# Attention feeding a feed-forward block: the first two chunks interleaved, the weights decoded in that order, GpSimd's early work given to TensorE and VectorE

## The chip, the core and the metric

The kernel runs on one core of one Trainium2 chip. The metric is the device time of one execution in microseconds (us). A core has five engines with an instruction stream each: TensorE (PE in the profile, its weight loads PEld), VectorE (DVE), ScalarE (ACT), GpSimd (POOL) and SyncE (SP), which here issues the transfers from and to memory (DMA). They wait for one another through semaphores. SBUF is the on-chip memory; PSUM is the memory that matmuls write, eight banks of 128 partitions by 2 KB.

## The reference

```python
# q, k, v: [8 batches, 8 heads, 576 positions, 64], float32
q_d, k_d, v_d = (a.reshape(B, H, 144, 4, D).mean(axis=3) for a in (q, k, v))
out_up = np.repeat(sm_attn(q_d, k_d, v_d), 4, axis=2)          # "down": pooled attention
mask = np.abs(pos[:, None] - pos[None, :]) < 4                 # "local": 7 neighbours
attn = softmax(np.where(mask, scale * q @ k.T, -1e9))
x = (out_up + attn @ v).transpose(0, 2, 1, 3).reshape(4608, 512)
h = x @ w_in                                                   # 512 x 2048
g = np.maximum(h, 0.0) + alpha * np.minimum(h, 0.0)
out = g @ w_out                                                # 2048 x 512
```

The weights `w_in`, `w_out` and `alpha` are float64 in memory.

## The kernel before

**Feed-forward part.** The 4608 tokens are cut into 18 chunks of 256. Each chunk has 8 steps, of 256 of the 2048 hidden columns each, so that there are 144 steps; step 8c+i is part i of chunk c. `h_step` computes h in a `ps_h` bank with 24 matmuls of 128x256 (each operand is split in a high and a low part: xh·wih, xh·wil, xl·wih). ScalarE (`t`, L651) and VectorE (`t`, L654) apply the two slopes, ScalarE copies the high part `gh` (L656), GpSimd subtracts to get the low part `gl` (L97). `out_step` adds 12 matmuls of 128x512 into two output banks (L690) that stay with the chunk for its 8 steps, and are then copied by ScalarE to `sg` and stored. h steps run two ahead of out steps (`AH = 2`); `t`, `gh` and `gl` have two buffers each. In this text "t8" is the VectorE part of step 8, and so on.

**Weights.** A float64 arrives as two int32 words. `decode` turns a 128x512 piece into a float32 (`temp`): Abs on ScalarE, then on VectorE a clamp (L153), a shift (L154) and two combining operations (L155, L156). ScalarE then writes the high part (`wih`, `woh`), and the low part is a subtraction (`wil`: VectorE L210, or GpSimd L97 for 5 of 16 pieces by `POOL_LO`; `woh` and `wol` with a sign, VectorE L204). `load_weights` walks four groups n of 512 hidden columns, w_in before w_out in each: 32 pieces. Group 3 is late: its buffers come free when the attention of batch 0 is done.

**Attention.** Batch 0 is done up front by `pair(hp)` for four pairs of heads, with the scores on TensorE. Batches 1 to 7 run in the shadow of the feed-forward steps, as units u = 3 to 23 of 192 tokens. `local(u)` multiplies shifted k by q and reduces, on VectorE (L551, L553), from a copy `qp` of q in PSUM bank q (copied by ScalarE, L548); it keeps the probabilities and the running sum `lb` in PSUM bank l, and multiplies by v and adds (L596, L598), which gives `x`; then come transposes on TensorE, an addition of the pooled part (`xf`) and the split in high and low parts. `down(b, hp)` is the pooled attention of a pair of heads: loads `ld` (three buffers), additions on GpSimd (L100), small matmuls and softmax.

**PSUM.** `ps_o` 2 banks (output sums), `ps_h` 2, q 1, l 1, d 2.

**Order.** The program is written chunk by chunk, with as many attention steps issued between two feed-forward steps as the tokens need that are wanted next; a list scheduler then sets the order on each engine by readiness in its own timeline, with priorities (`high_priority`: the work behind h by `HP`, `pair` by `PP`, decode by `DP`). On an engine instructions run strictly in that order. Transfers are issued by SP in its own order, each waiting for its buffer.

## Time and profile before

| | us |
|---|---|
| runs | 1144.88, 1130.85, 1134.6 |
| median | 1134.6 |
| profiled execution, its own time | 1138.52 |
| its span in the profile | 1136.7 |

| engine | busy us | share of the span |
|---|---|---|
| PE | 1005.7 | 88% |
| DVE | 861.4 | 76% |
| POOL | 526.4 | 46% |
| ACT | 454.7 | 40% |

The mean granted TensorE clock of the profiled execution is 0.926. From 359 us on TensorE is busy 734.65 of 777.7 us. The first t runs at 111.9 us; by 359 us the weights are decoded and the first 27 steps or so have begun. In the timeline t8 begins at 178.7, t16 at 251.0 and t24 at 320.4 us; unit 3's products begin at 160.7 us, unit 4's at 224.7 us. A row of the windows view gives, for a stretch, each engine's busy us with the number of instructions, the granted clock, the DMA share and GB/s. In a timeline row stand start, duration, engine, line, operation, output<-inputs, size, and in brackets how long the engine had been idle and for whom.

### The profile page before, as it was taken

To read this page: it belongs to the slowest core of one execution; us is meant where nothing else is said; L and a number is where in the kernel's file an instruction comes from. 1 tells how busy PE (TensorE), PEld (TensorE's weight loads), DVE (VectorE), ACT (ScalarE), POOL (GpSimd) and SP (SyncE) were. 2 spreads that over 40 slices of the span, in tenths; PEclk is the share of its full clock that TensorE was granted. 3 is DMA by queue.
4 is the path that set the end of the run, shared out by engine and by line. 5 is a ranking of instruction groups with operands and counts; after the bars stand their busy time and mean duration, and the time that the engine had idled before them with its cause. 6 is when DMAs were issued, how large, how long until landed. Compare 5 with 4: busy or idle time off the path is not lost.

```text
span 1136.7 us, 17891 instructions
## 1 busy us (share of the span) xinstructions
PE 1005.7 (88%) x6402; PEld 879.8 (77%) x6402; DVE 861.4 (76%) x1467; ACT 454.7 (40%) x1223; POOL 526.4 (46%) x633
## 2 busy tenths in 40 slices
PE   5857797898768999889999999989999989999995
PEld 5646675696657898777888888878888878899994
DVE  7999496597847889678878988779887778895110
ACT  5767344242323443333444334344343425333221
POOL 4787474333434644544555543555537244333221
PEclk9756889798968999899999999999999989999998
DMA  8944612222222222221223222323222212100000
GB/s 181 240 150 145 189 43 86 65 83 76 66 92 77 87 100 87 92 87 65 80 95 109 85 80 89 105 76 101 88 92 82 96 58 78 54 19 19 1 20 19
DMA packets 57503, 98.26 MB, mean 86 GB/s; under 512 B 19910, under 2 KB 25286, under 8 KB 57414
## 3 DMA queue, kind: packets, MB, share of 16 engines
q1 hardware_dynamic: 57414, 97.12, 27.1%
q8 instruction: 50, 0.82, 0.3%
q14 instruction: 39, 0.32, 0.1%
HBM read 87.67 MB, written 9.44 MB: 85 GB/s over the span
## 4 chain that ended last, share of the span: by engine, by line
PE 53%; DMA 20%; DVE 11%; POOL 6%; SPq 4%; issue 3%; ACT 2%; ACTq 0%; POOLq 0%; DVEq 0%
PE o L690 26%; PE h L642 22%; DMA ldk<-in_k 10%; DMA q<-in_q 4%; DMA ldq<-in_q 3%; POOL gl L97 2%; SPq L348 2%; DVE temp L155 1%; SPq L499 1%; POOL ldv L100 1%; DVE temp L153 1%; PE pv L266 1%; DVE temp L156 1%; PE xp L607 1%; DMA raw<-in_moe_w_out 1%
## 5 line engine op out<-in xcount | busy, mean ns | idle before, releaser
L97 POOL TENSOR_TENSOR gl<-t,gh 128x512 fp32r<-128x512 f32 x144 | 187.0, 1301 | 238.5 <-ACT gh L656 221.3
L654 DVE SCALAR_TENSOR_TENSOR t<-h,sign,t 128x256 f32<-128x256 f32 x288 | 125.6, 478 | 165.1 <-ACT t L651 159.3
L690 PE MATMUL o<-woh,gl 128*128 128x512 f32 x576 | 193.7, 414 | 45.1 <-POOL gl L97 45.0
L651 ACT ACTIVATE t<-h,slope 128x256 f32<-128x256 f32 x288 | 120.3, 469 | 244.4 <-PE h L642 159.4
L642 PE MATMUL h<-xh,wih 128*128 128x256 f32 x1152 | 201.1, 291 | 1.0 <-DVE t L654 0.7
L690 PE MATMUL o<-woh,gh 128*128 128x512 f32 x576 | 190.2, 407 | 10.3 <-ACT gh L656 10.3
L642 PE MATMUL h<-xh,wil 128*128 128x256 f32 x1152 | 194.3, 288 | 1.0 <-DVE wil L210 1.0
L690 PE MATMUL o<-wol,gh 128*128 128x512 f32 x576 | 191.2, 409 | 0.0
L642 PE MATMUL h<-xl,wih 128*128 128x256 f32 x1152 | 188.0, 285 | 0.0
L642 PEld LDWEIGHTS h<-xh,wih 128*128 128x128 f32 x1152 | 174.0, 196 | 14.4 <-DVE t L654 2.4
L690 PEld LDWEIGHTS o<-woh,gl 128*128 128x128 f32 x576 | 110.4, 195 | 75.8 <-POOL gl L97 51.7
L642 PEld LDWEIGHTS h<-xh,wil 128*128 128x128 f32 x1152 | 163.1, 194 | 1.9 <-DVE wil L210 1.2
L642 PEld LDWEIGHTS h<-xl,wih 128*128 128x128 f32 x1152 | 159.9, 192 | 0.3
L656 ACT CAST gh<-t 128x512 fp32r<-128x512 f32 x144 | 89.4, 621 | 148.5 <-PE o L690 78.6
L551 DVE TENSOR_TENSOR qk<-k,qp 128x768 f32<-128x768 f32 (+1 forms) x126 | 135.0, 1081 | 0.0
L553 DVE TENSOR_REDUCE ls<-qk 128x12 f32<-128x768 f32 (+1 forms) x126 | 133.5, 1080 | 0.2
L690 PEld LDWEIGHTS o<-wol,gh 128*128 128x128 f32 x576 | 111.1, 195 | 24.9 <-issue 0.2
L690 PEld LDWEIGHTS o<-woh,gh 128*128 128x128 f32 x576 | 102.3, 194 | 25.2 <-ACT gh L656 10.5
L598 DVE TENSOR_TENSOR lb<-lb,pv 128x384 f32<-128x384 f32 x210 | 117.9, 562 | 4.0
L100 POOL TENSOR_TENSOR ldk<-ldk 72x256 f32<-72x256 f32 x56 | 45.2, 808 | 153.7 <-DMA ldk<-in_k 143.3
L596 DVE TENSOR_TENSOR pv<-v,lb 128x1152 f32<-128x1152 f32 x84 | 96.8, 1152 | 2.5
L100 POOL TENSOR_TENSOR ldq<-ldq 72x256 f32<-72x256 f32 x56 | 42.8, 774 | 80.6 <-DMA ldq<-in_q 80.4
(146 smaller groups left out, 1194.3 us busy)
## 6 DMA issues: line engine op xcount, KB each, us to landing
k<-in_k SPq DMA_DIRECT2D x41, 384.0 KB
v<-in_v SPq DMA_DIRECT2D x41, 384.0 KB
raw<-in_moe_w_in SPq DMA_DIRECT2D x16, 512.0 KB
raw<-in_moe_w_out SPq DMA_DIRECT2D x16, 512.0 KB
ldq<-in_q SPq DMA_DIRECT2D x56, 144.0 KB
ldk<-in_k SPq DMA_DIRECT2D x56, 144.0 KB
ldv<-in_v SPq DMA_DIRECT2D x56, 144.0 KB
q<-in_q SPq DMA_DIRECT2D x42, 192.0 KB
```

The source lines that it names most:

```text
L97: nc.gpsimd.tensor_tensor(o, a, b, op=ALU.subtract)
L100: nc.gpsimd.tensor_tensor(o, a, b, op=ALU.add)
L348: nc.sync.dma_start(qk[hp][:, i, :, e, :], bass.AP(src.tensor, (2 * hp + e) * HEAD, [[512, 72], [64, 8], [1, 64]]))
L551: nc.vector.tensor_tensor(pr[:, :nd], window(kt, half, d0, nd), qp.unsqueeze(1).to_broadcast([128, nd, 2, 192]), op=ALU.mult)
L553: nc.vector.tensor_reduce(out=s[:, half, d0:d0 + nd, :].rearrange("p a b -> p (a b)"), in_=pr[:, :nd].rearrange("p a h (t d) -> p (a h t) ...
L596: nc.vector.tensor_tensor(pr[:, :nd], window4(vt, half, d0, nd), prob(half, d0, nd), op=ALU.mult)
L598: nc.vector.tensor_tensor(acc, acc, pr[:, i], op=ALU.add)
L642: nc.tensor.matmul(ph[:, j], w[:, m, 128 * o:128 * o + 128], x[:, m, :], start=(i == 0), stop=(i == 11))
L651: nc.scalar.activation(t[:, j], ph[:, j], AF.Copy, scale=slope[:, f:f + 1])
L654: nc.vector.scalar_tensor_tensor(t[:, j], ph[:, j], sign[:, f:f + 1], t[:, j], op0=ALU.mult, op1=ALU.max)
L656: nc.scalar.copy(gh, t)
L690: nc.tensor.matmul(po, g[:, j, 128 * m:128 * m + 128], wo[w][n][:, o, :], start=(f == 0 and i == 0), stop=(f == NF - 1 and i == 2))
```

## The change

**Order of steps.** `PAIRED = 2`: the steps run 0, 8, 1, 9, 2, 10, ..., 7, 15, and from 16 on as before. Both chunks use each piece of weight when it is there. Chunk 1's two output sums need banks of their own meanwhile: they are put in banks q and l, which units' `local` uses too. Unit 3 (`UB = {3: 'sx'}`) reads q straight from SBUF in its products, without a copy in bank q; its `lb` stays in bank l.

**Weights.** Loaded and decoded by step, 256 hidden columns at a time, in the order in which the steps ask for them: w_in piece 0 (`i0`), w_out piece 0 (`o0`), `i1`, `o1`, ... Pieces 0 to 5 are made with batch 0's attention, 6 and 7 late. Three raw buffers are used in turn. A w_in transfer now has runs of 2 KB (256 float64), before 4 KB. All `wil` subtractions are VectorE's. `HOLD = 5`: the first three `ld` transfers of the downs come behind a tiny VectorE copy that reads `wol` of piece 5.

**Batch 0's attention.** The sums over 4 neighbours of q and k (VectorE for two pairs, GpSimd for two) and of v (GpSimd) become accumulating matmuls: 16 instead of 4 transposes for q and k, 16 instead of 4 for the pooled product with v, per pair; the v tiles get four buffers. The multiplication of the probabilities with 1/sum (128x630) and the low part of x (8 pieces of 128x256 or so) move from GpSimd to VectorE. The fourth pair's exp is done like the other three's (subtract on VectorE, one exp on ScalarE, reduce on VectorE). `GATE`, small VectorE copies that delayed raw loads, is gone. All pairs have priority 1, and the decode none.

The diff, cut to its core (removed code that the functions above show is left out):

```diff
@@ -46,31 +46,21 @@
...
-FQ = 'vvpp'
-FV = 'pppp'
-FSUB = 'vvvv'
-FMUL = 'pppp'
-FLO = 'pppp'
-FEXP = 'vvva'
-SEQ = '00001111'
-UB = {}
-GATE = (-1, -1, 2, 3)
+UB = {3: 'sx'}
...
-DP = (1, 100, 1, 1)
-PP = (1, 1, 250, 250)
-POOL_LO = (1, 5, 1, 1)
-ORDER = 'a0 w w a1 w w a2 b0 w w a3 b1 w w b2 b3'
-WIDE = ()
+PP = (1, 1, 1, 1)
+ORDER = 'a0 i0 a1 o0 a2 i1 b0 a3 b1 o1 i2 b2 b3'
+PAIRED = 2
+HOLD = 5
...
+    raws, turns = {}, [0, 0]
+    weights_temp = []
+
+    def load_raw(which, fp):
+        n = fp // 2
+        if which == 1 and n == 3:
+            pool, tag, bufs = pools[0], ("prod", "vt")[fp % 2], 2
+            raw = [pool.tile([128, 1, 512, 2], I32, tag=tag, name=f"raw1_{fp}{c}", bufs=bufs) for c in range(2)]
+        elif which == 1:
+            t = one.tile([128, 2, 512, 2], I32, tag=f"slot{turns[0] % 3}", name=f"raw1_{fp}")
+            raw = [t[:, c:c + 1] for c in range(2)]
+        else:
+            slot = turns[0] % 3 if n < 3 else 2 + fp % 2
+            t = one.tile([128, 2, 2, 256, 2], I32, tag=f"slot{slot}", name=f"raw0_{fp}")
+            raw = [t[:, c] for c in range(2)]
+        turns[0] += 1
+        src = (w_in, w_out)[which].bitcast(I32)
+        for c in range(2):
+            if which == 0:
+                nc.sync.dma_start(raw[c].rearrange("p k a b -> p k (a b)"),
+                                  bass.AP(src.tensor, 256 * c * 2 * DF + 512 * fp, [[2 * DF, 128], [256 * DF, 2], [1, 512]]))
+            else:
+                row = 256 * fp + 128 * c
+                nc.sync.dma_start(raw[c].rearrange("p k a b -> p (k a b)"), src[row:row + 128, :])
+        raws[which, fp] = raw
+
+    def weight_tiles(which, n):
+        if n == 0 or (wi, wo)[which][0][n] is not None:
+            return
+        w = (wi, wo)[which]
+        for i, x in enumerate("hl"):
+            tag = f"slot{2 * which + i}" if n == 3 else f"spare{8 - 4 * n + 2 * which + i}"
+            w[i][n] = one.tile([128, 4, 512], F32R, tag=tag, name=f"w{'io'[which]}{x}{n}")
+
+    def make(which, fp):
+        n, half = divmod(fp, 2)
+        if not weights_temp:
+            weights_temp.append(one.tile([128, 4, 512], I32, tag="slot3", name="temp"))
+        weight_tiles(which, n)
+        w = (wi, wo)[which]
+        for c, raw in enumerate(raws.pop((which, fp))):
+            if n < 3:
+                t = weights_temp[0][:, turns[1] % 4]
+            else:
+                t = pools[0].tile([128, 512], I32, tag=("x", "xf")[turns[1] % 2], name=f"temp{which}{fp}{c}")
+            turns[1] += 1
+            hi, lo = raw[:, :, :, 1], raw[:, :, :, 0]
+            if which == 0:
+                t = t.rearrange("p (k a) -> p k a", k=2)
+                wh, wl = (w[i][n][:, 2 * c:2 * c + 2, 256 * half:256 * half + 256] for i in range(2))
+                decode(t, hi, lo)
+                nc.scalar.copy(wh, f32(t))
+                nc.vector.tensor_tensor(wl, f32(t), f32(wh), op=ALU.subtract)
+            else:
+                t = t.rearrange("p (k a) -> p k a", k=1)
+                f = 2 * fp + c
+                wh, wl = (w[i][n][:, f % 4:f % 4 + 1] for i in range(2))
+                decode(t, hi, lo)
+                sg = sign[:, f:f + 1]
+                nc.scalar.activation(wh, f32(t), AF.Copy, scale=sg)
+                nc.vector.scalar_tensor_tensor(wl, f32(t), sg, f32(wh), op0=ALU.mult, op1=ALU.subtract)
 
...
+                if held:
+                    nc.vector.tensor_copy(ld[:, 0, 0, 0:1], held.pop())
                 nc.sync.dma_start(ld.rearrange("p g f d -> p (g f d)"),
...
-            vt[hp] = st.tile([72, 2, 8, 64], F32, tag="vt", name=f"fv{hp}", bufs=2)
+            vt[hp] = st.tile([72, 2, 8, 64], F32, tag="vt", name=f"fv{hp}", bufs=4)
...
-                            nc.tensor.transpose(ps[:, (2 * x + g) * 72:(2 * x + g) * 72 + 72], sums[x][:, g],
-                                                ident[:72, :72])
+                            o = ps[:, (2 * x + g) * 72:(2 * x + g) * 72 + 72]
+                            for t in range(4):
+                                nc.tensor.matmul(o, qk[hp][:, x, 4 * g + t].rearrange("p h d -> p (h d)"), ident[:72, :72],
+                                                 start=(t == 0), stop=(t == 3))
...
             if EM[hp] == "b":
                 th = yield from down_probs(0, hp, sd)
             mx = one.tile([128, NWIN], F32, tag="lmx", name=f"fmx{hp}")
             sm = one.tile([128, NWIN], F32, tag="lsm", name=f"fsm{hp}")
...
-            ENG[FMUL[hp]].tensor_tensor(p, p, rs.unsqueeze(2).to_broadcast([128, NWIN, KEYS]), op=ALU.mult)
+            nc.vector.tensor_tensor(p, p, rs.unsqueeze(2).to_broadcast([128, NWIN, KEYS]), op=ALU.mult)
...
-                    nc.tensor.matmul(po[r, 0:144].rearrange("p (b a) -> p b a", b=3), vd[:, g, 64 * e:64 * e + 64],
-                                     pr, start=(g == 0), stop=(g == 1))
+                    for t in range(4):
+                        nc.tensor.matmul(po[r, 0:144].rearrange("p (b a) -> p b a", b=3), vt[hp][:, e, 4 * g + t, :],
+                                         pr, start=(g == 0 and t == 0), stop=(g == 1 and t == 3))
...
-                    ENG[FLO[hp]].tensor_tensor(lo, xs, f32(hi), op=ALU.subtract)
+                    nc.vector.tensor_tensor(lo, xs, f32(hi), op=ALU.subtract)
...
     def new_outs(c):
-        if c == 1 and SEQ != "00001111":
+        if 0 < c < PAIRED:
             outs[c] = outs.get(c) or [bank(kind, f"o1_{kind}") for kind in "ql"]
...
+        todo = [(w, fp) for fp in range(NP) for w in range(2)]
         for step in ORDER.split():
-            if step == "w":
...
-        while next(wl) != "late":
-            pass
+        for fp in range(NP - 2):
+            for which in range(2):
+                if (which, fp) not in raws:
+                    load_raw(which, fp)
+                make(which, fp)
...
+    for which in range(2):
+        for fp in (NP - 2, NP - 1):
+            load_raw(which, fp)
+    for which in range(2):
+        for fp in (NP - 2, NP - 1):
+            make(which, fp)
+    held.extend(f32(wo[1][HOLD // 2][0:72, 2 * (HOLD % 2) + 1, c:c + 1]) for c in range(LDB))
...
+    order = [NP * c + fp for fp in range(NP) for c in range(PAIRED)] + list(range(PAIRED * NP, NS))
+    for c in range(PAIRED):
+        new_outs(c)
```

Three places of the instruction order. The numbers behind names count tiles; `h8_1936` is h of step 8, `qk3_05` unit 3's product of half 0.

First, VectorE in the middle of unit 3. Before:

```order
L551 TENSOR_TENSOR qk3_05_1257<-k3_1199,qp3_0_1209 128x768
L156 SCALAR_TENSOR_TENSOR temp321_1099<-raw321_1096,temp321_1099 128x512
L654 SCALAR_TENSOR_TENSOR t7_1882<-h7_1857,sign_78,t7_1882 128x256 x2
L553 TENSOR_REDUCE ls3_1208<-qk3_05_1257 128x12
L204 SCALAR_TENSOR_TENSOR wol3_1075<-temp311_1088,sign_78,woh3_1074 128x512
L204 SCALAR_TENSOR_TENSOR wol3_1075<-temp321_1099,sign_78,woh3_1074 128x512
L551 TENSOR_TENSOR qk3_10_1278<-k3_1199,qp3_1_1276 128x1152
L153 TENSOR_SCALAR temp331_1108<-temp331_1108 128x512
L654 SCALAR_TENSOR_TENSOR t8_1961<-h8_1936,sign_78,t8_1961 128x256 x2
```

After, the end of unit 3 and the t's behind it:

```order
L578 TENSOR_TENSOR pv3_11_1541<-v3_1253,lb3_1397 128x1152
L580 TENSOR_TENSOR lb3_1397<-lb3_1397,pv3_11_1541 128x384 x3
L578 TENSOR_TENSOR pv3_14_1562<-v3_1253,lb3_1397 128x768
L281 TENSOR_REDUCE dnb1_3_1659<-s1_3_1655 96x3
L580 TENSOR_TENSOR lb3_1397<-lb3_1397,pv3_14_1562 128x384 x2
L582 TENSOR_TENSOR x3_1442<-lb3_1397,pv6_3_1_1425 128x2x3x64
L287 RECIPROCAL drs1_3_1661<-dsm1_3_1660 96x3
L634 SCALAR_TENSOR_TENSOR t3_1859<-h3_1834,sign_78,t3_1859 128x256 x2
L634 SCALAR_TENSOR_TENSOR t11_1930<-h11_1905,sign_78,t11_1930 128x256 x2
L597 TENSOR_TENSOR xf3_0_1741<-xp3_0_1736,od1_1235 128x4x4x16
L597 TENSOR_TENSOR xf3_0_1741<-xp3_0_1736,od1_1235 128x2x4x16 x2
L634 SCALAR_TENSOR_TENSOR t4_2007<-h4_1982,sign_78,t4_2007 128x256 x2
```

Unit 3's first products (`qk3_05`, `qk3_10`) had t7 and t8 and decode operations among them. Now all of unit 3, up to `x3` of both halves, stands ahead of t3, t11 and t4, and the decode is over before it.

Second, TensorE at the first out step of chunk 1 that uses bank l. Before, the sums of step 8 (`o1_0`, `o1_1`):

```order
L642 MATMUL h12_2233<-xh1_382,wih2_930 128x256 x4
L642 MATMUL h12_2233<-xh1_382,wil2_932 128x256
L690 MATMUL o1_0_2122<-woh0_82,gh8_1962 128x512
L690 MATMUL o1_0_2122<-wol0_83,gh8_1962 128x512
L690 MATMUL o1_0_2122<-woh0_82,gl8_1963 128x512
L690 MATMUL o1_0_2122<-woh0_82,gh8_1962 128x512
L690 MATMUL o1_0_2122<-wol0_83,gh8_1962 128x512
L690 MATMUL o1_1_2123<-woh0_82,gh8_1962 128x512
```

After:

```order
L251 MATMUL qkT1_3_1600<-ident_73,s2k1_3_1582 128x72 x2
L262 MATMUL s1_3_1655<-kd1_3_1653,qd32_84 96x144 x3
L670 MATMUL o1_l_1166<-woh0_82,gh8_1227 128x512
L670 MATMUL o1_l_1166<-wol0_83,gh8_1227 128x512
L670 MATMUL o1_l_1166<-woh0_82,gl8_1228 128x512
L670 MATMUL o1_l_1166<-woh0_82,gh8_1227 128x512
L670 MATMUL o1_l_1166<-wol0_83,gh8_1227 128x512
```

Step 8's out matmuls stood behind h11 and part of h12. Now the second half of them (`o1_l`) stands behind the small matmuls of the fourth `down`, and the h steps behind it in the same stream; `o1_l` takes the bank that `lb3` had.

Third, ScalarE where unit 4's q is copied (`qp4_0`, to bank q). Before:

```order
L656 CAST gh8_1962<-t8_1961 128x512
L203 ACTIVATE woh3_1074<-temp331_1108,sign_78 128x512
L651 ACTIVATE t9_2038<-h9_2013,slope_79 128x256 x2
L548 COPY qp4_0_1769<-q4_1342 128x384
L281 ACTIVATE dp1_3_1614,dsm1_3_1612<-s1_3_1607,dnb1_3_1611 96x144 x3
L283 ACTIVATE dsm1_3_1612<-dsm1_3_1612 96x3
L287 ACTIVATE dp1_3_1614<-dp1_3_1614,drs1_3_1613 96x144 x3
```

After:

```order
L675 COPY sg0_0_2614<-o0_0_1163 128x512
L675 COPY sg0_1_2617<-o0_1_1164 128x512
L631 ACTIVATE t17_2668<-h17_2643,slope_79 128x256 x2
L636 CAST gh17_2669<-t17_2668 128x512
L675 COPY sg1_0_2689<-o1_q_1165 128x512
L675 COPY sg1_1_2692<-o1_l_1166 128x512
L530 COPY qp4_0_1817<-q4_1390 128x384
L631 ACTIVATE t18_2767<-h18_2742,slope_79 128x256 x2
L636 CAST gh18_2768<-t18_2767 128x512
```

`qp4_0` stood behind t9. Now it stands behind t17 and behind the copies `sg1_0` and `sg1_1` of chunk 1's finished sums, of which the first is the last reader of bank q.

More of the change, by code (lines that the diff above doesn't have):

```diff
@@ L100, in add @@
         nc.gpsimd.tensor_tensor(o, a, b, op=ALU.add)
+    NS = NCHUNK * NF // 2
+    NP = NF // 2
     ident = const.tile([128, 128], F32, name="ident")
@@ L145, in tile_attention_moe, with decode @@
             w[i][0] = const.tile([128, 4, 512], F32R, name=f"{name}{x}0")
-    def decode(dst, raw):
-        hi, lo = raw[:, :, :, 1], raw[:, :, :, 0]
+    def decode(dst, hi, lo):
         nc.scalar.activation(f32(dst), f32(hi), AF.Abs)
@@ L216, in tile_attention_moe @@
     od = {}
+    held = []
     qd32 = const.tile([128, 3, 96], F32, name="qd32")
```

113 lines of the change are left out of this document (11 added, 102 removed).

## Prediction

> **What bounds the kernel now.** I read the page's row of transfers first (GB/s in 40 slices of 28.4 us), then a windows view cut at t0, unit 3, unit 4, t24 and 359 us.
>
> ```profile
> GB/s 181 240 150 145 189 43 86 65 83 76 66 92 77 87 100 87 92 87 65 80 95 109 85 80 89 105 76 101 88 92 82 96 58 78 54 19 19 1 20 19
> ```
>
> ```profile
> 13.40:111.90 98.50, 68.89 (x450) 57.16 (x449) 96.82 (x164) 66.32 (x186) 68.64 (x52) 0.69 0.68 177
> 111.90:160.70 48.80, 38.09 (x210) 32.10 (x211) 32.26 (x46) 20.07 (x50) 30.43 (x35) 0.79 0.45 143
> 160.70:224.70 64.00, 50.08 (x292) 42.04 (x292) 42.83 (x71) 22.95 (x63) 25.33 (x27) 0.87 0.21 71
> 224.70:320.40 95.70, 83.82 (x518) 73.53 (x517) 80.55 (x133) 32.93 (x88) 37.37 (x49) 0.93 0.22 75
> 320.40:359.00 38.60, 23.85 (x135) 20.80 (x134) 17.15 (x35) 11.13 (x36) 16.20 (x23) 0.73 0.23 78
> 359.00:1136.70 777.70, 734.65 (x4772) 648.11 (x4770) 586.62 (x1008) 295.99 (x794) 340.64 (x421) 0.98 0.22 73
> ```
>
> (Columns: stretch and length, then PE, PEld, DVE, ACT, POOL busy, clock, DMA share, GB/s.) From 359 us TensorE is busy 734.65 of 777.7 us (94%): what comes sooner or later to t24 goes on to the end nearly whole. Up to t0 VectorE is full (96.82 of 98.5), so the start is VectorE's. Between, neither is full, and waits decide. From some steps behind t24 on the order on the engines is the same in both kernels. So I predict when t24 (320.4 us) comes, in five stages.
>
> **A: up to t0.** VectorE's decode operations side by side, as a timeline and as groups:
>
> ```profile
> 13.40 0.43 DVE L153 TENSOR_SCALAR temp<-temp 128x512 f32<-128x512 f32 x1 [2.94 <-ACT temp L152]
> 13.87 0.43 DVE L154 TENSOR_SCALAR temp<-temp 128x512 int32<-128x512 int32 x1
> 14.33 0.69 DVE L155 SCALAR_TENSOR_TENSOR temp<-raw,temp 128x512 int32<-128x512 int32 x1
> 15.42 0.68 DVE L156 SCALAR_TENSOR_TENSOR temp<-raw,temp 128x512 int32<-128x512 int32 x1
> 16.83 1.28 POOL L97 TENSOR_TENSOR wil<-temp,wih 128x512 fp32r<-128x512 f32 x1 [4.31 <-ACT wih L206]
> 16.93 1.73 DVE L155 SCALAR_TENSOR_TENSOR temp<-raw,temp 128x512 int32<-128x512 int32 x1
> 18.80 0.65 DVE L442 TENSOR_TENSOR fp<-fs,fmx 128x490 f32<-128x490 f32 x1
> 22.36 0.68 DVE L210 TENSOR_TENSOR wil<-temp,wih 128x512 fp32r<-128x512 f32 x1
> 22.96 0.41 DVE L410 TENSOR_TENSOR fs2q<-fqk 72x256 f32<-72x256 f32 x1
> 23.29 0.80 DVE L451 TENSOR_REDUCE fsm<-fp 128x9 f32<-128x630 f32 x1
> 114.41 0.74 DVE L204 SCALAR_TENSOR_TENSOR wol<-temp,sign,woh 128x512 fp32r<-128x512 f32 x1
> ```
>
> ```profile
> L153 DVE TENSOR_SCALAR temp<-temp 128x512 f32<-128x512 f32 x32 | 22.6, 709 | 11.3 <-ACT temp L152 11.3
> L154 DVE TENSOR_SCALAR temp<-temp 128x512 int32<-128x512 int32 x32 | 22.8, 713 | 0.3
> L155 DVE SCALAR_TENSOR_TENSOR temp<-raw,temp 128x512 int32<-128x512 int32 x32 | 27.4, 857 | 0.2
> L156 DVE SCALAR_TENSOR_TENSOR temp<-raw,temp 128x512 int32<-128x512 int32 x32 | 27.5, 864 | 0.1
> L204 DVE SCALAR_TENSOR_TENSOR wol<-temp,sign,woh 128x512 fp32r<-128x512 f32 x16 | 15.0, 950 | 8.2 <-ACT woh L203 8.2
> L210 DVE TENSOR_TENSOR wil<-temp,wih 128x512 fp32r<-128x512 f32 x11 | 10.9, 995 | 0.0
> ```
>
> L155 took 0.69 alone and 1.73 when it began 0.10 us behind a GpSimd operation of 1.28. The groups sum to 126.2 us. At the single durations they would be 32 x (0.43+0.43+0.69+0.68) + 16 x 0.74 + 11 x 0.68 = 90.7. The excess of 35.5 us is what GpSimd at its side costs. In the new order GpSimd has nothing between its first masks and gl0, so this excess goes for the 24 of 32 pieces that are made before t0: 35.5 x 24/32 = 27; I take 24, since some of the excess comes behind t0.
>
> Added to VectorE: four 128x630 multiplications (0.65 x 630/490 = 0.84 each, 3.4), eight low parts (0.48 each by t's group below, 3.8), five wil (0.68 each, 3.4), the fourth pair's subtractions and reduce against its two small scalings (0.65 + 0.3 + 0.80 against 0.8, net 1), and the last operations of piece 5, that now stand ahead of t0 (4). Gone: the sums of q and k, four at 0.7 and four at 0.41 (4.4). So VectorE's work is 96.8 - 24 + 15.6 - 4.4 = 84. TensorE's 96 added small matmuls (24 per pair; at 0.27, the cold L293 row under D, 26 us) lie in the 29.6 us in which it idled up to t0; uncovered, they are in the upper bound.
>
> Transfers can hold this up. Up to the fifth weight piece and the windows' copies some 10.1 MB must land (pairs 3.54, copies 1.29, five pieces of 1.05, from the shapes): 5.1 in the first slice at 181 GB/s and 5.0 at 240, 49 us. The 58 VectorE instructions ahead of that piece take 27 us, to 40.4. I put the wait at 10 (0 to 15, which takes in shorter runs). t0 at 13.4 + 84 + 10 = **107** (97 to 112).
>
> **B: t0 to unit 3.** Work is 32.26 in the second window. The last w_in raw tiles wait for buffers and a transfer of some 10 us (the q row of the chain, under D), as now; GpSimd's share is smaller. I take **32** (26 to 40), to 139 (before 160.7).
>
> **C: unit 3.** All of it now stands ahead of t3.
>
> ```profile
> 160.70 1.34 DVE L551 TENSOR_TENSOR qk<-k,qp 128x1152 f32<-128x1152 f32 x1
> 224.66 1.35 DVE L551 TENSOR_TENSOR qk<-k,qp 128x1152 f32<-128x1152 f32 x1
> 320.43 0.86 DVE L654 SCALAR_TENSOR_TENSOR t<-h,sign,t 128x256 f32<-128x256 f32 x2
> 321.21 0.23 DVE L561 TENSOR_TENSOR ls<-ls,mask_l 128x84 f32<-128x84 f32 x1
> ```
>
> ```profile
> L654 DVE SCALAR_TENSOR_TENSOR t<-h,sign,t 128x256 f32<-128x256 f32 x288 | 125.6, 478 | 165.1 <-ACT t L651 159.3 <-POOL gl L97 1.7 <-POOL s2v L100 1.4
> L598 DVE TENSOR_TENSOR lb<-lb,pv 128x384 f32<-128x384 f32 x210 | 117.9, 562 | 4.0
> L561 DVE TENSOR_TENSOR ls<-ls,mask_l 128x84 f32<-128x84 f32 x7 | 6.4, 907 | 0.1
> ```
>
> From unit 3's first product to unit 4's, VectorE was busy 42.83 us (third window). Less eight t's (t5 to t12, 0.88 the pair: 7.0), plus three additions that were still to come (1.7), that is 37.5. Waits inside, 2. The products now read both operands from SBUF. The mask addition L561 does that too: 0.23 us alone, 0.907 in the mean, 0.68 more; for six products, 4. This gives 43.5; I take **42** (37 to 50), to 181. The Trainium skill ("SBUF — State Buffer", section "SBUF: two separate sides") says that a VectorE instruction with two SBUF inputs and a GpSimd instruction that reads SBUF lock each other out, the later one waiting for the whole of the other. That speaks against this edit: by the rule each product could wait a whole GpSimd operation (1.28, six make 7.7), 3.7 more than by the L561 row; the L155 row of 1.73 agrees that the wait can be long.
>
> **D: x3 to unit 4.** Bank l is lb3's until x3 is done, and `o1_l` of step 8 waits for it. gh8 and gh9 stay occupied, so h2 and h3 are the last that can run beside unit 3, and TensorE idles. Behind x3 it is the bound, and VectorE idles: unit 4's `qp4_0` waits in bank q for chunk 1's end (the ScalarE rows).
>
> ```profile
> 1068.37 2.80 PE h L642 x24
> 1071.17 2.79 PE o L690 x12
> 112.03 10.13 DMA q<-in_q
> 320.17 12.06 DMA ldk<-in_k
> ```
>
> ```profile
> 143.23 0.53 PE L293 MATMUL pT<-ident,dp 96*72 96x96 f32 x2 [9.29 <-ACT dp L287]
> 143.47 0.78 PE L690 MATMUL o<-wol,gh 128*128 128x512 f32 x1
> 148.63 0.87 PE L642 MATMUL h<-xh,wih 128*128 128x256 f32 x4
> ```
>
> ```profile
> L100 POOL TENSOR_TENSOR ldk<-ldk 72x256 f32<-72x256 f32 x56 | 45.2, 808 | 153.7 <-DMA ldk<-in_k 143.3 <-DVE pv L596 9.8 <-PE h L642 0.6
> ```
>
> Left then are the l halves of steps 8 and 9 (12 matmuls, 2.8), 12 out steps and 10 h steps of 2.8, in all 64.4, and 3 for transposes and downs. A slow clock after the wait: behind the 9.29 us at 143.23 the 12 out matmuls up to 148.63 took 5.16, 2.4 more than 2.79; I add that. gl2 stands on GpSimd behind additions of three `ld` tiles, whose transfers stand in SP's queue behind v5, which waits for unit 3's last reads of v. Six additions of about 0.8 and the transfers lie between 3.5 (already there) and 12; I take 8. Sum 64.4 + 3 + 2.4 + 8 = **77** (70 to 84): unit 4 starts at 258, before 224.66.
>
> **E: unit 4 to t24.** The fourth window: 80.55 busy in 95.7. Five t's less (six stand there now, eleven did: 4.4), and unit 3's rest is gone (three additions 1.7, its x and xf some 2.2): 72, and 5 of the 15 us of waits, since loads and downs had 60 us to run ahead. **77** (72 to 92, where all waits return). t24 at 335.
>
> **Sum.** 107 + 32 + 42 + 77 + 77 = 335 against 320.4: +15 on the profiled execution's 1138.52 (span 1136.7), which stands 4 above the median. On the median 1134.6 that is 1149.
>
> **Rivals.**
>
> Faster: all of the start's gain is kept. t0 at 97 (no wait for transfers; 27 of contention gone), B 28, C 38, D 72, E 73: t24 at 308, 12 earlier. Also the pause behind t24 goes:
>
> ```profile
> 334.20 0.88 DVE L654 SCALAR_TENSOR_TENSOR t<-h,sign,t 128x256 f32<-128x256 f32 x2 [12.13 <-ACT t L651]
> ```
>
> The window 320.4 to 359 has 14.75 us without TensorE; if loads that arrive early end it, -14 more: -26, 1109. For it: VectorE's 98% up to t0, and GpSimd wholly free. Against: 181 GB/s in the first slice.
>
> Slower: D is held by GpSimd's queue. If v5 (10.13 as for q) and then the `ld` transfers (12.06) run one after the other, with six additions (4.8), gl2 comes 27 us behind x3, not 8: out step 2 and all behind it wait. +19: t24 at 354, 1134.6 + 34 = 1169. It decides from the point where the ldq tiles land later than 10 us behind x3. For it: GpSimd's additions idled 143.3 us for ldk. Against: in D the transfers have the queue nearly alone.
>
> No net effect: the gain at the start is given back and no more. 107 + 32 + 38 + 70 + 72 = 319: 1134. This takes unit 3 without contention and gl2 without a wait.
>
> **How the numbers follow.** Forecast 0.45, faster rival 0.22, slower 0.23, no effect 0.10. The forecast's own range is 1130 to 1165. A measurement tells about 2% from no change: below 1112 or above 1157. Faster by that: 0.7 of the faster rival, 0.16. Slower: the slower rival, and 0.3 of the forecast above 1157, 0.36. The rest 0.48. The range of 1102 to 1176 takes in the rivals but for a quarter to a third of each at its far side, some 0.13, and 0.05 of things not thought of.
>
> **What would show it.** A: t0 at 97 to 112, and L153 to L156 near 0.43 and 0.69 in the mean; if they stay at 0.71 and 0.86, GpSimd was not the cause. Transfers: VectorE's idle before L153, for raw. C: no t for some 40 us, TensorE idle, L551 of unit 3 longer than 1.35. D: VectorE idle for some 60 us with TensorE near full; gl2 beginning 8 (forecast) or 27 us (slower rival) behind x3. E: t24 at 335, and the rest of the span as before (816 us behind t24). The prediction is wrong if TensorE does other useful work in C, if D is under 60, or if the span behind t24 differs by more than 10.

## The result, and the profile after

| | before | after | ratio, 95% interval |
|---|---|---|---|
| median, us | 1132.72 | 1198.72 | 1.058 (1.0502 to 1.0658) |
| span of the profiled execution, us | 1136.7 | 1202.5 | |

The change made the kernel 66 us slower. The forecast, 1149 with a range of 1102 to 1176, had the direction of its likeliest case right and the size wrong by a factor of over four (14 us for 66). Times here and below are medians of runs in the fast state, which leaves out one run of e3 (1308.14 us).

The windows view of the changed kernel, cut where the prediction cut it: first t, first product of unit 3, the first out matmuls that run on after the pause, first product of unit 4, t24, end. Columns as in the prediction: stretch and length; PE, PEld, DVE, ACT, POOL busy; clock, DMA share, GB/s.

```profile
13.40:124.90 111.50, 101.42 (x635) 90.16 (x635) 82.82 (x176) 62.63 (x154) 0.00 (x0) 0.94 0.52 139
124.90:168.70 43.80, 31.84 (x201) 28.82 (x199) 29.04 (x46) 14.85 (x30) 20.16 (x22) 0.91 0.52 156
168.70:243.00 74.30, 23.66 (x94) 15.67 (x94) 37.77 (x60) 19.66 (x66) 34.71 (x49) 0.52 0.28 92
243.00:312.60 69.60, 69.28 (x433) 61.18 (x434) 13.15 (x31) 25.95 (x63) 26.33 (x29) 0.95 0.07 21
312.60:398.90 86.30, 54.00 (x317) 46.74 (x316) 74.78 (x114) 22.01 (x60) 24.55 (x34) 0.76 0.23 79
398.90:1202.50 803.60, 757.19 (x4904) 668.20 (x4902) 603.18 (x1040) 307.04 (x825) 354.35 (x440) 0.97 0.22 73
```

The reader sees three things. Up to the first t TensorE is full now (101.42 of 111.5), and VectorE is not (82.82). From 168.7 us on TensorE nearly stops for 74 us (23.66 busy). Then the two take turns: for 69.6 us TensorE is full and VectorE idles (13.15), and for 86.3 us VectorE is busy for 74.78 and TensorE idles a third of the time. With unit 3's last sum at 226.7 us (shown below) the stages are:

| stage | before | forecast | measured |
|---|---|---|---|
| A: first t at | 111.9 | 107 | 124.9 |
| B: to unit 3 | 48.8 | 32 | 43.8 |
| C: unit 3 until its last sum | | 42 | 58.0 |
| D: to unit 4 | | 77 | 85.9 |
| E: to t24 | 95.7 | 77 | 86.3 |
| t24 at | 320.4 | 335 | 398.9 |
| from t24 to the end | 816.3 | 816 | 803.6 |

Every stage came out 9 to 18 us longer than forecast, 64 in all; the stretch behind t24 gave 13 back.

**Stage A.** Groups of TensorE's instructions up to the first t, first of the kernel before, then of the changed one (count, busy us, mean ns).

```profile
L467 PE MATMUL fdv<-th,fvd 72*64 72x144 f32 x32 | 5.0, 425 | 3.3 <-ACT th L296 3.3
L415 PE MATMUL fsum<-ident,fs2k 72*128 72x72 f32 x8 | 1.8, 335 | 0.0
L415 PE MATMUL fsum<-ident,fs2q 72*128 72x72 f32 x8 | 1.7, 311 | 4.3 <-POOL fs2q L410 2.3 <-DVE fs2q L410 2.0
```

```profile
L411 PE MATMUL fsum<-ident,fqk 72*128 72x72 f32 x128 | 28.9, 419 | 0.0
L449 PE MATMUL fdv<-th,fv 72*64 72x144 f32 x128 | 20.1, 378 | 0.0
```

The 8.5 us of before became 49.0. The trace has 256 instructions where 48 stood: a float32 matmul shows as two of them, a transpose as one.

And VectorE's decode, groups of the changed kernel over the whole run:

```profile
L148 DVE SCALAR_TENSOR_TENSOR temp<-raw,temp 128x512 int32<-128x512 int32 x32 | 24.2, 761 | 0.1
L147 DVE SCALAR_TENSOR_TENSOR temp<-raw,temp 128x512 int32<-128x512 int32 x32 | 23.3, 732 | 0.3
L145 DVE TENSOR_SCALAR temp<-temp 128x512 f32<-128x512 f32 x32 | 15.6, 488 | 29.6 <-ACT temp L144 29.5
L146 DVE TENSOR_SCALAR temp<-temp 128x512 int32<-128x512 int32 x32 | 14.8, 466 | 0.3
```

They are the clamp, shift and two combinations that took 0.71, 0.71, 0.86 and 0.86 in the mean before. Up to the first t alone, where GpSimd does nothing, they took 0.42, 0.42, 0.68 and 0.68, the single durations that the prediction named as the sign. VectorE's relief came, but TensorE now set the pace: from 30 to 90 us it was busy without a break, while VectorE was busy 42.1 of these 60 us. Only from 105 us on was VectorE full again (18.25 of 19.9), with decode that stood behind the pairs' work in its stream.

**Stages C and D.** The chain of waits between the first t and 245 us, then TensorE's and VectorE's timelines from 164 us, those instructions that had waited and their neighbours (in brackets how long, and for whom).

```profile
131.43 19.15 DMA raw<-in_moe_w_in
...
204.84 14.24 DMA ldk<-in_k
...
231.01 8.88 DMA ldq<-in_q
...
242.04 1.23 POOL gl L87
```

```profile
164.39 0.90 PE L262 MATMUL s<-kd,qd 128*96 128x144 f32 x6
178.56 1.17 PE L295 MATMUL pT<-ident,dp 96*72 96x96 f32 x6 [13.27 <-ACT dp L289]
...
221.07 0.50 PE L251 MATMUL qkT<-ident,s2k 72*128 72x72 f32 x2 [13.54 <-POOL s2k L90]
222.54 1.75 PE L262 MATMUL s<-kd,qd 128*96 128x144 f32 x6 [0.96 <-ACT kd L257]
226.72 0.80 PE L670 MATMUL o_l<-woh,gh 128*128 128x512 f32 x1 [2.43 <-DVE x L582]
...
243.32 1.22 PE L670 MATMUL o<-woh,gl 128*128 128x512 f32 x2 [9.59 <-POOL gl L87]
```

```profile
197.35 0.56 DVE L575 TENSOR_TENSOR lb<-v,lb 128x384 f32<-128x384 f32 x1 [3.91 <-DMA v<-in_v]
...
224.33 0.60 DVE L281 TENSOR_REDUCE dnb<-s 96x3 f32<-96x432 f32 x1 [15.11 <-PE s L262]
224.85 1.15 DVE L580 TENSOR_TENSOR lb<-lb,pv 128x384 f32<-128x384 f32 x2
226.11 0.56 DVE L582 TENSOR_TENSOR x<-lb,pv 128x384 f32<-128x384 f32 x1
```

From 164.39 us, just behind the last h matmul, to 226.72 us TensorE's stream has only the four downs' small matmuls, each waiting for the one before it through other engines, and at the end for an `ldk` transfer (14.24 us in the chain). The fourth down's reduce `dnb` stands in VectorE's stream ahead of unit 3's last additions. So unit 3 waits 15.11 us for the down, the out matmul `o_l` waits for unit 3's x in bank l, and gl waits on GpSimd behind the next down's `ldq`. That is one chain through four engines and the transfers.

### The profile page after: what moved, and what is told of

Read it like the earlier page. It is cut to its first block, busy times and chain, and to the rows that moved or that the text cites. A ratio compares the mean times of both kernels' runs of the same rounds, so it can differ in the third digit from the quotient of the medians.

```text
span 1202.5 us, 18252 instructions
## 1 busy us (share of the span) xinstructions
PE 1043.5 (87%) x6610; PEld 916.6 (76%) x6610; DVE 844.8 (70%) x1478; ACT 457.5 (38%) x1204; POOL 465.7 (39%) x596
## 4 chain that ended last, share of the span: by engine, by line
PE 56%; DMA 22%; DVE 7%; POOL 6%; issue 3%; SPq 3%; ACT 2%; ACTq 0%; POOLq 0%; DVEq 0%
PE o L670 23%; PE h L622 21%; DMA ldk<-in_k 10%; DMA ldq<-in_q 5%; DMA q<-in_q 3%; DMA raw<-in_moe_w_in 2%; PE fsum L411 2%; POOL gl L87 2%; PE fdv L449 1%; POOL ldv L90 1%; PE pv L268 1%; PE xp L589 1%; DVE qk L533 1%; PE fs L402 1%; DMA k<-in_k 1%
## 5 line engine op out<-in xcount | busy, mean ns | idle before, releaser
L670 PE MATMUL o<-woh,gl 128*128 128x512 f32 x544 | 181.2, 412 | 37.7 <-POOL gl L87 37.7
L670 PE MATMUL o<-wol,gh 128*128 128x512 f32 x544 | 178.5, 406 | 0.0
L670 PE MATMUL o<-woh,gh 128*128 128x512 f32 x544 | 177.2, 403 | 0.0
L670 PEld LDWEIGHTS o<-woh,gl 128*128 128x128 f32 x544 | 103.8, 194 | 66.5 <-POOL gl L87 43.2
L533 DVE TENSOR_TENSOR qk<-k,qp 128x768 f32<-128x768 f32 (+1 forms) x120 | 127.9, 1077 | 3.3 <-ACT qp L530 2.5
L670 PEld LDWEIGHTS o<-wol,gh 128*128 128x128 f32 x544 | 103.9, 192 | 23.5
L670 PEld LDWEIGHTS o<-woh,gh 128*128 128x128 f32 x544 | 95.2, 191 | 13.7 <-issue 0.6
```

The lines of the kernel that those rows point to most:

```text
L533: nc.vector.tensor_tensor(pr[:, :nd], window(kt, half, d0, nd), qp.unsqueeze(1).to_broadcast([128, nd, 2, 192]), op=ALU.mult)
L670: nc.tensor.matmul(po, g[:, j, 128 * m:128 * m + 128], wo[w][n][:, o, :], start=(f == 0 and i == 0), stop=(f == NF - 1 and i == 2))
```

## The experiments

Each run's time is a median beside runs of the kernel before on the same chip; the ratio is to these. The runs of the kernel before had medians of 1132.72 (beside after), 1135.58 (e1 to e4), 1137.38 (e5 to e8) and 1135.28 (e9 to e11), so a difference of a few us between runs of different groups says nothing.

| run | us | ratio to before, 95% | first t | unit 3 | unit 4 | t24 |
|---|---|---|---|---|---|---|
| before | 1132.72 | 1 | 111.9 | 160.7 | 224.7 | 320.4 |
| after | 1198.72 | 1.058 (1.0502 to 1.0658) | 124.9 | 168.7 | 312.6 | 398.9 |
| e1 sums off TensorE | 1186.95 | 1.0448 (1.04 to 1.0495) | 85.7 | 129.8 | 283.7 | 370.9 |
| e2 steps in old order | 1131.81 | 0.9942 (0.9912 to 0.9971) | 118.8 | 163.4 | 224.2 | 318.8 |
| e3 no held loads | 1171.05 | 1.0294 (1.0241 to 1.0348) | 127.5 | 168.2 | 279.9 | 367.5 |
| e4 unit 3's sum in SBUF | 1155.5 | 1.0173 (1.0125 to 1.0221) | 122.5 | 163.9 | 258.1 | 347.5 |
| e5 = e1 + e2 | 1095.19 | 0.9642 (0.9603 to 0.9681) | 90.8 | 137.7 | 191.9 | 286.4 |
| e6 = e5 + e3 | 1109.88 | 0.9767 (0.9725 to 0.981) | 102.7 | 153.6 | 194.7 | 297.1 |
| e7 before, GpSimd's work moved | 1121.4 | 0.9871 (0.9837 to 0.9906) | 99.7 | 157.5 | 213.4 | 313.3 |
| e8 = e1 + e3 + e4 | 1113.6 | 0.979 (0.9754 to 0.9826) | 103.2 | 156.8 | 214.9 | 302.9 |
| e9 = e1 + e4 | 1124.99 | 0.9898 (0.9864 to 0.9932) | 89.7 | 139.2 | 222.2 | 315.2 |
| e10 = e5, v sums on TensorE | 1111.68 | 0.9785 (0.9754 to 0.9816) | 102.2 | 143.5 | 203.1 | 303.8 |
| e11 before, interleaved alone | 1154.63 | 1.0175 (1.0132 to 1.0218) | 111.9 | 225.6 | 251.8 | 343.1 |

(The last four columns are starts in the profiled execution: first t, first products of units 3 and 4, t24. The order on VectorE differs between the kernels, so that the first t does not stand behind the same work in all of them.)

**e1: the sums off TensorE.**

```diff
+FQ = 'vvpp'
+FV = 'pppp'
...
+                        ENG[FQ[hp]].tensor_tensor(s4, lv[:, :, 0:256], lv[:, :, 256:512], op=ALU.add)
...
-                            for t in range(4):
-                                nc.tensor.matmul(o, qk[hp][:, x, 4 * g + t]...
+                            nc.tensor.transpose(ps[...], sums[x][:, g], ident[:72, :72])
```

> The changed kernel, but batch 0's sums over four neighbours are taken from TensorE again and made as before by VectorE (q, k of two pairs) and GpSimd (the rest); the v tiles have two buffers again. Theory (TensorE bounds the changed start): in the changed kernel TensorE was busy 101.4 of the 111.5 us before the first t, 49.0 of it in the new sums against 8.5 before; without them the first t comes near 112 instead of 124.9 us, and the time falls by 10 to 15, to about 1186. Rival (decode and transfers bound the start): the first t stays at 125 or comes later, because GpSimd is again beside the decode, and the time stays at 1199 or rises by up to 10.

The windows of its start, its pause and the stretch behind it:

```profile
13.40:85.70 72.30, 59.51 (x421) 47.80 (x421) 71.62 (x152) 54.98 (x144) 29.87 (x17) 0.74 0.70 195
...
129.80:217.00 87.20, 24.90 (x106) 15.85 (x106) 37.11 (x61) 19.47 (x65) 43.56 (x52) 0.54 0.24 81
217.00:283.70 66.70, 66.68 (x421) 59.52 (x422) 13.03 (x31) 25.56 (x62) 26.07 (x28) 0.98 0.07 22
```

The first t came at 85.7 us, 39 earlier, not 13: VectorE is the bound again (71.62 of 72.3), with the decode free of most of GpSimd. That is 26 us ahead of the kernel before, with the decode by step, the hold and GpSimd's moves all in it. Part of it is order: 72 decode operations (clamp, shift and two combinations) stand ahead of this first t, 93 in the changed kernel and 92 in the kernel before. But unit 3 starts 39 us earlier too (129.8 for 168.7). The time fell by 12 only, so that the 1186 of the expectation was met by luck: its gain at the start was three times too small, and the loss behind it was not foreseen. The pause grew from 74.3 to 87.2 us, since the loads did not come sooner by as much. Unit 3's wait for v, 3.91 us in the changed kernel, is 10.12 here:

```profile
169.34 0.56 DVE L591 TENSOR_TENSOR lb<-v,lb 128x384 f32<-128x384 f32 x1 [10.12 <-DMA v<-in_v]
```

Of the 39 us, 28 are left at t24 (370.9 for 398.9): 11 were lost in the same knot. From t24 to the end the profiled execution takes 810.1 us against 803.6, which loses 6.5 more. The rest of the way to 12 is that both profiled executions lie some us off their medians (1182.8 for 1186.95, 1204.35 for 1198.72).

**e2: steps in the old order.**

```diff
-UB = {3: 'sx'}
+UB = {}
-PAIRED = 2
+PAIRED = 1
```

> The changed kernel, but the steps run 0, 1, 2, ... as before: chunk 1's sums in the output banks, unit 3 and unit 4 with their banks q and l; the decode by step, the sums on TensorE and the rest of the change stay. Theory (the banks q and l lent to chunk 1 tie unit 3, unit 4 and TensorE to one another): the 62 us from 164 to 227 in which TensorE does only small matmuls, and VectorE's idle 70 us behind it, go; the start's loss of 13 stays; the time falls to 1140 to 1155. Rival (the loss comes from the order of weights and transfers): it stays above 1180.

```profile
163.40:224.20 60.80, 43.90 (x281) 37.68 (x280) 41.42 (x69) 24.15 (x70) 30.04 (x41) 0.86 0.28 93
224.20:318.80 94.60, 85.14 (x546) 73.83 (x546) 82.95 (x142) 39.65 (x113) 47.42 (x66) 0.95 0.28 95
```

Unit 3 to unit 4 takes 60.8 us with TensorE busy 43.9 beside it, where the changed kernel took 144. The 67 us that this gave are the whole loss, and more than expected (1140 to 1155). So the loss needs the interleaving with its banks; e3, e4 and e8 show what else it needs. The slow start (first t at 118.8 us) is made good by t24 (318.8 against 320.4).

**e3: no held loads.**

```diff
-    held.extend(f32(wo[1][HOLD // 2][0:72, 2 * (HOLD % 2) + 1, c:c + 1]) for c in range(LDB))
```

> The changed kernel, but the first three loads of the downs are not held back. Theory (the downs' loads, begun late, hold TensorE's stream in unit 3): the fourth down's scores, that came 15 us late for VectorE at 209 us, and gl2, that came 15 us behind x3, come earlier, and the time falls by 15 to 25, to about 1180. Rival (the bank alone): TensorE waits for x3 whatever the downs do; the time stays within 8 of 1199. Second rival (the loads take room from the weights' transfers): the first t comes later, and the time rises.

```profile
208.11 0.79 PE L670 MATMUL o_l<-woh,gh 128*128 128x512 f32 x1 [5.67 <-DVE x L582]
```

TensorE waits at `o_l` for x itself now, 18.6 us sooner than in the changed kernel (226.72), and no longer for the fourth down. Unit 3 from its first product to its last sum, in the changed kernel and here:

```profile
168.70:226.70 58.00, 16.64 (x72) 10.47 (x72) 37.73 (x60) 17.39 (x61) 27.66 (x38) 0.50 0.26 89
168.20:208.10 39.90, 11.91 (x65) 8.01 (x65) 37.84 (x59) 10.95 (x36) 22.30 (x21) 0.60 0.26 88
```

The columns are those of the windows above. VectorE does as much work in both (37.73 and 37.84 us); it waits 20 us in the first and 2 in the second. 28 us came back: the late loads of the downs were a part of the knot, and that is a little more than the theory's 15 to 25.

**e4: unit 3's sum out of PSUM.**

```diff
-UB = {3: 'sx'}
+UB = {3: 'ss'}
...
+        if UB.get(u, "xx")[1] == "s":
+            lb = two.tile([128, 512], F32, tag="stage", name=f"lb{u}", bufs=SB)
```

> The changed kernel, but unit 3's probabilities and running sum lie in SBUF (a buffer of the output staging) and not in bank l. Theory (bank l): step 8's second half no longer waits for x3; t3 to t5 and t10 to t13 run inside unit 3; TensorE's pause from 164 to 227 shrinks to about half, and the time falls by 25 to 40, to about 1165. What is left of the loss is unit 4's wait for bank q. Rival (downs ahead of the out matmuls in TensorE's stream and their late loads): the pause stays, and the time stays within 10 of 1199.

```profile
163.90:210.00 46.10, 42.66 (x256) 36.77 (x255) 45.75 (x62) 20.13 (x55) 28.11 (x26) 0.93 0.21 70
210.00:258.10 48.10, 32.71 (x192) 27.22 (x192) 8.83 (x21) 15.90 (x48) 25.78 (x39) 0.88 0.30 99
```

In unit 3 both engines work at once (42.66 and 45.75 of 46.1). The pause is gone, not halved. What stays is VectorE's idle 39 us from 210 to 258, while unit 4 waits for bank q; TensorE too is idle for 15 us there, most of it (9.4 us before 221.54) for a down's GpSimd addition behind an `ldk` transfer. 43 us of the 66 hung on bank l.

**e5: old order of steps, and the sums off TensorE** (the edits of e1 and e2).

> The changed kernel with both undone: steps in the old order, and batch 0's sums taken from TensorE again. What stays of the change is the decode by step, all wil, the multiplication and the low part of x on VectorE, the fourth pair's exp and the held loads. Theory (in the interleaved order the earlier start was eaten by the banks; in the old order it goes on to the end): the first t comes near 86 us as without the TensorE sums, 33 earlier than in the old order with them, and the time falls from 1132 by 25 to 33, to 1100 to 1107. Rival (late weights and unit 3's loads hold t5 to t10 whatever the start is): half of it is lost, 1115 to 1120.

```profile
13.40:90.80 77.40, 61.53 (x435) 50.30 (x434) 75.63 (x158) 57.06 (x148) 23.56 (x17) 0.74 0.71 191
...
191.90:286.40 94.50, 87.28 (x557) 75.83 (x556) 81.55 (x136) 38.47 (x109) 46.81 (x64) 0.95 0.30 97
```

Without the knot the start's gain reaches the end: first t 28 us earlier than in e2, t24 32 earlier, the time 37 less. This is the fastest kernel of the study, 3.6% under the kernel before, and better than the theory's 1100 to 1107. What it keeps of the change is the decode by step, the moves from GpSimd to VectorE, the fourth pair's exp and the held loads. e6 and e7 price the held loads and the moves; no run separates the rest.

**e6: the same without held loads** (the edit of e3 on e5).

> As the run before, and the first three loads of the downs are not held back. Theory (the hold only hurt where the downs stood ahead of the out matmuls): within 6 of the run before. Rival (early loads take room and GpSimd time from the start): 8 to 15 slower, with the first t later.

```profile
13.40:102.70 89.30, 65.65 (x453) 53.41 (x452) 83.83 (x160) 59.44 (x162) 58.48 (x44) 0.69 0.71 186
```

The rival was right: 15 us slower. GpSimd is busy 58.48 us beside the decode against 23.56 in e5; two VectorE instructions more stand ahead of the first t, but 8 us more of busy time. Nearly all of it is decode: 76 decode operations took 50.5 us where 75 took 43.1 in e5. VectorE also waited 5.4 us for one `temp` of ScalarE (0.7 in e5). So the hold pays at the start mainly by keeping the downs' additions away from the decode, and costs in the interleaved order (e3), where the downs stand ahead of the out matmuls.

**e7: before, with GpSimd's work moved to VectorE alone.**

```diff
-FMUL = 'pppp'
-FLO = 'pppp'
+FMUL = 'vvvv'
+FLO = 'vvvv'
-POOL_LO = (1, 5, 1, 1)
+POOL_LO = (0, 0, 0, 0)
```

> The kernel before, with one part of the change alone: all wil subtractions, the multiplication of the probabilities and the low part of x of batch 0 moved from GpSimd to VectorE (10.6 us of single durations). Theory (GpSimd beside the decode costs VectorE about as much as the work itself): the first t stays within 6 of 111.9, the operations of the decode get shorter in the mean, and the time stays within 10 of 1134. Rival (VectorE was full, so work given to it adds up): the first t 10 later, 1145. Rival (the contention is the larger): the first t 8 to 15 earlier, 1120 to 1126.

```profile
13.40:99.70 86.30, 61.89 (x446) 51.23 (x445) 85.42 (x165) 60.14 (x174) 42.17 (x36) 0.70 0.69 184
```

```profile
L154 DVE TENSOR_SCALAR temp<-temp 128x512 int32<-128x512 int32 x32 | 16.6, 519 | 0.2
```

GpSimd's busy time before the first t fell from 68.64 to 42.17 us, VectorE's from 96.82 to 85.42. Not all of that is contention: the order moved too, and 81 decode operations (L153 to L156) stand ahead of this first t where 92 did. The whole run, with the same work in both, is the fair comparison; before, then e7:

```profile
PE 1005.7 (88%) x6402; PEld 879.8 (77%) x6402; DVE 861.4 (76%) x1467; ACT 454.7 (40%) x1223; POOL 526.4 (46%) x633
PE 990.3 (88%) x6402; PEld 869.1 (78%) x6402; DVE 855.4 (76%) x1484; ACT 454.8 (41%) x1223; POOL 499.0 (45%) x616
```

VectorE took over 17 instructions and its busy time fell by 6.0 us. The shift operation L154 went from 0.713 to 0.519 us in the mean. The second rival held: first t 12 us earlier, time 16 below the runs beside it. How much of the two is contention and how much order, no run separates.

**e8: interleaved and repaired** (the edits of e1, e3 and e4).

> The changed kernel, interleaved, with the three that helped together: sums off TensorE, unit 3's sum in SBUF and no held loads. If the three losses are separate, they add up: 1199 - 12 - 43 - 23 = 1121; with the whole of the earlier start (39) kept as well, 1094. If they are one and the same wait, it stays near the best of them alone, 1150. Unit 4's wait for bank q stays in any case.

1113.6, near the sum of the three (1198.7 - 11.8 - 27.7 - 43.2 = 1116). It looks as if the losses were separate, but e9 below shows that this is luck: e1 and e4 together give 19 us more than their sum, and e3 on top of them 11 where it gave 28 alone. The interleaved kernel is now 2.1% (1.7 to 2.5) below the kernel before. Its counterpart in the old order, e6, is ahead in t24 (297.1 against 302.9); in time (1109.88 against 1113.6) the two are not clearly apart, since their runs overlap. So without the held loads the interleaving costs little once bank l and the sums are mended; with them it costs 30 us (e9 against e5, 1124.99 for 1095.19). In neither case does it gain.

**e9: as e8, with the held loads.**

> As the interleaved and repaired kernel, but with the first three loads of the downs held back as in the changed kernel. In the old order of steps the hold brought the first t from 102.7 to 90.8 us and the time from 1110 to 1095. Theory (the hold spares the start the downs' additions on GpSimd beside the decode): the same here, first t at 88 to 92, time 1114 - 12 = 1102, still above the old order's 1095 for unit 4's wait for bank q. Rival (with the interleaving, held loads come late for unit 3 whatever bank its sum is in): the first t is early and the time is not, 1110 to 1125.

```profile
196.82 0.80 PE L689 MATMUL o_q<-woh,gl 128*128 128x512 f32 x1 [11.64 <-POOL gl L91]
...
217.22 0.79 PE L689 MATMUL o_q<-woh,gl 128*128 128x512 f32 x1 [10.68 <-POOL gl L91]
```

The rival was right: the first t comes 13.5 us sooner than in e8, and the time is 11 us longer. Twice TensorE waits 11 us for a gl on GpSimd, with bank l out of the way; both gl stand behind additions of `ld` tiles whose transfers were late (GpSimd waits 16.82 us for an `ldv` and 8.01 for an `ldq`). The slower rival of the prediction is seen here by itself. The time is 1125 where e1 and e4 would add up to 1144: with bank l out of the way the start's gain is no longer lost in the knot.

**e10: old order, v sums on TensorE.**

```diff
+                    for t in range(4):
+                        nc.tensor.matmul(po[r, 0:144]..., vt[hp][:, e, 4 * g + t, :], pr, ...
```

> Old order of steps, q and k sums made by VectorE and GpSimd as before, but the v sums left with TensorE (128 matmuls, 20.1 us in the changed kernel). The run without any sums on TensorE had its first t at 90.8 and took 1095. Theory (TensorE bounds the start only when both are on it: 101 of 111 us with both, about 76 with this one): the first t stays within 5 of 91, and the time within 6 of 1095, or is better, since GpSimd has less. Rival (fp32 matmuls of the sums stand in the chain from pair to pair however many they are): the first t 8 to 12 later, 1103 to 1107.

```profile
13.40:102.20 88.80, 76.34 (x531) 66.59 (x531) 86.00 (x180) 61.05 (x153) 13.53 (x8) 0.73 0.68 177
```

16.5 us slower than e5, more than the rival said. But TensorE is not full here (76.34 of 88.8); VectorE is (86.00), with 180 instructions ahead of the first t where e5 has 158, 94 of them decode where e5 has 75. The scheduler put more ahead of it. How much of the 16.5 is the TensorE sums and how much this order stays open.

**e11: before, interleaved alone.**

```diff
-SEQ = '00001111'
+SEQ = '01010101'
```

> The kernel before with one part of the change alone: the steps of the first two chunks interleaved two by two, chunk 1's sums in banks q and l; weights, GpSimd's work and unit 3 as before. Theory (the banks are what costs): the first t stays at 112, unit 3's products begin only when chunk 1's sums are out of bank q, VectorE idles meanwhile, and the time is 1165 to 1200. Rival (the loss of the changed kernel needs the late weights and the sums on TensorE): within 15 of 1134.

```profile
225.65 2.22 DVE L551 TENSOR_TENSOR qk<-k,qp 128x1152 f32<-128x1152 f32 x2 [7.83 <-ACT qp L548]
```

Here the chunks alternate two steps at a time, not one by one as in the changed kernel. The direction is the theory's, the size (19 us) is below its 31 to 66 and nearer to the rival's 15. Unit 3 waits for bank q until 225.65 us, and VectorE idles till then (55.90 us busy of the 113.7 from the first t on), but TensorE is busy 101.73 of these 113.7: 16 steps run through nearly without a pause. Interleaving alone thus makes the engines wait in turn; the changed kernel's 74 us with little of TensorE need more, and e3 and e4 point to unit 3 and the downs in the middle of the paired steps.

## Why the prediction was wrong

**A, failed.** The step that failed is "TensorE's 96 added small matmuls (24 per pair; at 0.27, ... 26 us) lie in the 29.6 us in which it idled". There were 208 added instructions and 40.5 us (49.0 - 8.5). That is more than the 29.6 us of cover, and TensorE became the bound: first t at 124.9, above the range's end of 112. That upper end was said to take in the 26 us uncovered, but it left 5 for them. The price of 0.27 was also that of a transpose (L293), which is one instruction; the group of 32 `fdv` for 16 calls in the code could have shown that a float32 matmul is two. VectorE's term was right: 82.82 busy against the 84 worked out. e7 confirms the mechanism behind it: GpSimd beside the decode costs VectorE more than the work that it takes off it (861.4 to 855.4 us with 17 instructions more). The transfers (10 us) did not bind: ScalarE's waits for raw tiles up to the first t, 12.4 us in all and at most 1.9 at once, lay under TensorE's work.

**B, failed in its wait.** 43.8 for 32. I took VectorE's work (32.26) and nothing for a wait. The work was 29.04, but VectorE waited 12.45 us for the late w_in tiles:

```profile
144.31 0.43 DVE L145 TENSOR_SCALAR temp<-temp 128x512 f32<-128x512 f32 x1 [12.45 <-ACT temp L144]
```

The last of their transfers took 19.15 us in the chain where I put "some 10". The stage is as long without the sums on TensorE (e1, 44.1), in the old order (e2, 44.6) and nearly so without the hold (e3, 40.7); what would shorten it no run shows.

**C, failed.** The step that failed is "Waits inside, 2". I priced unit 3 by VectorE's work (37.5), these waits, and contention of its products in SBUF (4). The work was right: VectorE was busy 37.73 of the 58.0 us, with the contention in it. ("The decode is over before it" was wrong: the last decode operation ends at 191 us, in the middle of unit 3.) The six products tell how much contention there was:

```profile
L533 DVE TENSOR_TENSOR qk<-k,q 128x768 f32<-128x768 f32 x4 | 4.4, 1098 | 0.0
L533 DVE TENSOR_TENSOR qk<-k,q 128x1152 f32<-128x1152 f32 x2 | 2.9, 1471 | 0.0
```

Against 0.944 and 1.345 in the mean of the changed kernel's other units, the six lost 0.9 us together. The Trainium skill ("SBUF — State Buffer", "SBUF: two separate sides") states a lock between a VectorE instruction with two SBUF inputs and a GpSimd instruction that reads SBUF; the prediction's 7.7 us went by it. The decode's two-input operations agree with it (L155 0.857 to 0.786 in e7, when GpSimd does less). These products met it little, although GpSimd was busy for 12.35 of the 19.5 us in which they ran; why, no run shows. The missing 16 us were waits: for v (3.91) and for the fourth down's scores (15.11). I had read that `o1_l` stands behind the downs' matmuls in TensorE's stream, and `dnb` ahead of unit 3's last additions in VectorE's, both in rows that I showed, and I followed neither back to the downs' loads, which the hold had made late. e3 (-28) shows the loads' part: without the hold unit 3 takes 39.9 us with 2 of waits, as forecast. e4 (-43) shows the bank's.

**D, right in mechanism.** TensorE's 64.4 + 3 + 2.4 stands against 69.28 busy. gl2 came 15.3 us behind unit 3's x (226.7 to 242.0), not 8, and not the slower rival's 27. (The terms in the prediction add up to 77.8, not 77.)

**E, mis-sized.** 86.3 with VectorE busy 74.78 (I had 72): 11.5 us of waits, not 5. What I did not say is that D and E belong together: in D VectorE idles, and its work that could have run there makes TensorE idle in E. (This is a reading of the windows; no run tests it by itself.)

**Behind t24.** 803.6 for 816, by more than the 10 that I allowed: the stretch gave 12.7 back. In e2, with the old order of steps, it is 805.1 (1123.9 - 318.8), and in e7, which changes the start alone, 807.1 (1120.4 - 313.3). So it is not the interleaving. In the thirteen profiles here the stretch is 803.6 to 816.3 us, and the kernel before, from which I took my number, has the longest. Four runs of that kernel lie 15 us apart (1130.02 to 1144.88), so part of the 12.7 may be the spread of one kernel; the rest stays open.

**The rivals.** The slower rival's chain (v5, then `ld`, then GpSimd, then gl) was there, at 7 of its added 19 us; the faster rival's start (97) was possible, as e1 shows (85.7), but not with the sums on TensorE. I gave 0.36 to slower by over 2%, which came; A and C, with 18 and 16 us, are the largest parts of what I missed.

## What to carry to other kernels

Work that is moved to an engine because it has idle time must be counted in that engine's own instructions, from a group of the trace that does the same thing, not from the calls in the code; here 96 added calls were 208 added instructions and made a new bound.
When two streams share a buffer (bank l), follow what stands in front of the waiting instruction on its engine, all the way to the transfers: the price of the wait is that chain's, not the work of the owner.
Undo the parts of a change one by one when it fails: here a gain of 3.6% was inside a loss of 5.8%.

## What the runs showed of the hardware that was not expected

A float32 matmul of TensorE stands in the trace as two instructions (128 for 64 calls, 0.42 and 0.38 us each at the sizes 72x72 and 72x144), a float32 transpose by the identity of the same size as one (8 for 8 calls, 0.31 to 0.34 us). The chain of the changed kernel's start shows what that costs end to end, where the instructions follow on one another:

```profile
28.10 4.17 PE fsum L411 x20
42.92 0.48 PE f1T L382 x4
```

That is 0.42 us for a float32 matmul (two instructions of 0.21) against 0.12 for a transpose of the same 72x72 size, 3.5 times as much, both at a granted clock of 1.00. The Trainium skill ("FP8 and Floating Point Precision", section "TensorE Precision Notes") states four passes through the array for true float32, which is near this ratio; no run here separates the passes.

VectorE operations with a single SBUF input slow down beside GpSimd as well as those with two: the shift L154 was 0.43 us alone, 0.713 in the mean before, 0.519 with two fifths less GpSimd work up to the first t (e7) and 0.466 in the changed kernel. Work moved from GpSimd to a VectorE that was 98% busy up to the first t made VectorE's busy time shorter: 855.4 for 861.4 us over the whole run of e7, with 17 instructions more.
